# Pooled attention and mixture of depths on one core: steps of 256 tokens instead of 192, and the schedule rebuilt around them

## The chip, the core and the metric

The kernel runs on one core of a Trainium2 chip. The metric is the device time of one execution in microseconds (us), as the median of several runs. A profile of one execution is read beside it: for every engine it has each instruction with its start, its length and what the engine waited for. The engines are named as the profile names them: PE is TensorE's matmul and PEld its weight load, DVE is VectorE, ACT is ScalarE, POOL is GpSimd and SP is SyncE, which here only starts transfers. Each engine works through its own list of instructions in the order in which the program issues them.

## The reference

Eight batches are computed, each with eight heads, 576 tokens and 64 elements per head. The first half is attention against keys and values that were averaged over eight neighbouring tokens, so there are only 72 keys. The second half picks the 128 tokens of a batch with the highest gate score and puts those rows through two dense layers.

```python
def _attn_ref(q, k, v):                       # q, k, v: (8, 8, 576, 64) float32
    k_p = k.reshape(B, H, Sp, 8, D).mean(axis=3)          # Sp = 72
    v_p = v.reshape(B, H, Sp, 8, D).mean(axis=3)
    scores = scale * np.matmul(q, k_p.transpose(0, 1, 3, 2))
    attn = softmax(scores)                    # over the 72 keys
    return np.matmul(attn, v_p)               # bridged to x: (8, 576, 512)

def _moe_ref(x, w_gate, w1, w2, capacity):    # w1: (512, 1024), w2: (1024, 512), capacity 128
    scores = np.einsum('bsd,d->bs', x, w_gate)
    out = x.copy()
    for b in range(B):
        top_idx = np.argpartition(-scores[b], capacity)[:capacity]
        xe = x[b, top_idx]
        ye = np.maximum(xe @ w1, 0.0) @ w2
        g = 1.0 / (1.0 + np.exp(-scores[b, top_idx]))
        out[b, top_idx] = x[b, top_idx] + g[:, None] * ye
    return out
```

## The kernel before

The program has one path that does the work (`direct_path`) and a general one behind a flag, which these inputs do not take. The direct path cuts each batch into nine tiles of 64 tokens and walks through them in steps of three tiles (192 tokens), so there are three steps per batch and 24 in all. One output chunk has 128 rows, which is two tiles, so one step completes one or two chunks.

All matmuls are float32. In the trace one float32 matmul shows as two PE records, and the counts below are of records. Scores of one step: four row groups of 32 partitions, each with its own PSUM bank.

```python
def scores(u):
    b = u // NTH
    p = [bank(i, [128, 2, TS * TL]) for i in range(4)]
    for s in range(2):
        for j in range(2):
            for i in range(4):
                r = slice(32 * i, 32 * i + 32)
                nc.tensor.matmul(p[i][:, s, :], KT[b][r, j, s, :], QT[u][r, j, :, G * s : G * s + G], ...)
    ET[u] = [work.tile([128, 2, TS * TL], FT, name=f"et{i}", bufs=3) for i in range(4)]
    for i in range(4):
        nc.scalar.activation(ET[u][i], p[i], AF.Exp, scale=exp_scale)

def attend(a, heads=range(H)):                # one chunk: 8 heads x 2 tiles
    ...
            nc.tensor.matmul(PA[a][TL * t : TL * t + TL, g, E * n : E * n + E],
                             ET[u][h // 2][:, h % 2, TL * i : TL * i + TL], VP[u // NTH][:, h, :], ...)

def norm(a):                                  # DVE: reciprocal, scaled copy, gate parts
    nc.vector.reciprocal(rz, o[:, :, :, D])
    ...                                       # XS (rows to store, work.tile with 2 buffers), SS (gate parts)
```

Keys and values are pooled on POOL for all batches after the first. `VP` has two buffers, `vps[b % 2]`.

```python
def pool_v(b, g, eng):                        # eng is nc.gpsimd for b > 0
    eng.tensor_tensor(out=x[:, :, 0:4, :], in0=x[:, :, 0:4, :], in1=x[:, :, 4:8, :], op=OP.add)
    eng.tensor_tensor(out=x[:, :, 0:2, :], in0=x[:, :, 0:2, :], in1=x[:, :, 2:4, :], op=OP.add)
    eng.tensor_tensor(out=VP[b][:, h, 0:D], in0=x[:, :, 0, :], in1=x[:, :, 1, :], op=OP.add)
    nc.gpsimd.tensor_tensor(out=x[:, :, 2, :], in0=VP[b][:, h, 0:D], in1=wg[:, h, :], op=OP.mult)

def gate_v(b, g):                             # one more column of VP
    nc.vector.tensor_reduce(out=VP[b][:, h, D + 1], in_=VR[b, g][:, :, 2, :], axis=AX.X, op=OP.add)
```

The selection of a batch is a chain: `row_bcast` (PE), `count` (DVE), `one_hot` (PE, DVE), `gather` (PE, DVE, then an indirect DMA that POOL issues and that reads rows of `out` which the stores have put there), `x_trans` (PE), `hidden` in three parts, `finish` in three parts, and an indirect DMA from POOL that writes the rows back.

```python
def finish(b, part, nb):
    c = slice(176 * part, min(176 * part + 176, DM))
    for f in range(FB):
        nc.tensor.matmul(p, HT[b][:, f, :], w2[:, f, c], start=(f == 0), stop=(f == FB - 1))
    nc.scalar.activation(Y[b][:, c], p, AF.Copy, scale=g)
    nc.gpsimd.tensor_tensor(out=Y[b][:, c], in0=Y[b][:, c], in1=XR[b][:, c], op=OP.add)
    if part == 2:
        i = nc.gpsimd.indirect_dma_start(out=out_rows, out_offset=..., in_=Y[b], in_offset=None)
```

All loads and all stores are issued from SP. A table says in which slot of which step each job is issued; the pooling of the next batch ends one step before it is used, and the last part of `finish` is issued after it.

```python
    at(w + 5, 6, finish, b, 2, 1)             # w = 3 * (b + 1)
    if b + 1 < B:
        u = NTH * b
        at(u, 2, pool_k, b + 1, nc.gpsimd)
        at(u, 5, pool_v, b + 1, 0, nc.gpsimd)
        at(u + 1, 2, pool_v, b + 1, 1, nc.gpsimd)
        at(u + 1, 3, k_trans, b + 1)
        at(u + 2, 2, gate_v, b + 1, 0)
        at(u + 2, 3, gate_v, b + 1, 1)
    ...
for u in range(NU + 6):
    run(u, 0)
    ...                                       # attend and norm of the first chunk
    run(u, 1)
    if 0 < u < NU - 1:
        scores(u + 1)
    ...                                       # attend and norm of the second chunk
    run(u, 2)
    if u + 2 < NU:
        q_trans(u + 2)
    for slot in range(3, 8):
        run(u, slot)
```

Of the kernel before, what the change touches and what calls it, by code (L numbers as in the profile page):

```python
# [48 lines left out]
def direct_path(ctx, tc, q, k, v, moe_w_gate, moe_w1, moe_w2, moe_capacity, out, flag):  # L49
# [20 lines left out]

    nc = tc.nc
# [7 lines left out]
    NT = S // TL  # L79
    QT4 = TL // G  # L80
    TS = 3
    NTH = NT // TS
# [11 lines left out]
    NU = B * NTH  # L94
    NCH = B * NT // 2

# [20 lines left out]

    nc.vector.memset(vraws[0], 0.0)
    nc.gpsimd.memset(vraws[1], 0.0)
# [10 lines left out]
    load_q(0)  # L130
    load_v(0, 0)
# [23 lines left out]
    for t in kts + vps + vraws[2:]:  # L155
        nc.gpsimd.memset(t, 0.0)
    diff = counted("diff", [C, C], [[1, C]], 0, -1)
    part = counted("part", [C, 1], [[0, 1]], 0, 1)
    steps = counted("steps", [C, C // G - 1], [[-G, C // G - 1]], -G, 1)
    numbers = counted("numbers", [C, NC - 1], [[1, NC - 1]], 0, 0)  # L160
# [12 lines left out]
    auxb = [const.tile([C, NC, 5], BF, name=f"auxb{i}") for i in range(2)]  # L173
# [3 lines left out]
    def constants():  # L177
        nc.vector.tensor_scalar(ident, diff, 0.0, None, op0=OP.is_equal)
        nc.vector.tensor_scalar(before[:, NC - 2, :], diff, 0.0, None, op0=OP.is_lt)
        nc.vector.memset(ones, 1.0)  # L180
        nc.vector.memset(one32, 1.0)

        ge, q16, q4, hi = (const.tile([C, n], FT, name=x) for x, n in (
            ("ge", C // G - 1), ("q16", 1), ("q4", 1), ("hi", 1)))
        nc.vector.tensor_scalar(ge, steps, 0.0, None, op0=OP.is_ge, op1=OP.add, accum_out=q16)
        nc.vector.tensor_scalar(q4, q16, 4.0, None, op0=OP.mult)
        nc.vector.scalar_tensor_tensor(hi, q16, -float(G), part, op0=OP.mult, op1=OP.add)
        nc.vector.tensor_scalar(hi, hi, float(TG), None, op0=OP.mult)
        for i, a in enumerate(auxb):
            nc.vector.tensor_scalar(a[:, 0 : NC - 1, 0], numbers, 0.0, hi, op0=OP.mult, op1=OP.add)  # L190
            nc.vector.tensor_copy(a[:, NC - 1, 0:1], hi)
            nc.vector.tensor_scalar(a[:, i : i + NC - 1, 1], numbers, q4, None, op0=OP.add)  # L192
            h = (NC - 1) * (1 - i)
            nc.vector.tensor_scalar(a[:, h, 1:2], q16, float(32 - 4 * i), None, op0=OP.add)
# [10 lines left out]
    def bank(i, shape):  # L205

        return psum.tile(shape, FT, name=f"bank{i}", bufs=1)
# [22 lines left out]
    def pool_v(b, g, eng):  # L230
        x = VR[b, g]
        VP[b] = vps[b % 2]
        h = slice(HG * g, HG * g + HG)
        if eng is nc.vector:
            eng.tensor_reduce(out=VP[b][:, h, 0:D], in_=x.rearrange("p h t d -> p h d t"), axis=AX.X, op=OP.add)
        else:
            eng.tensor_tensor(out=x[:, :, 0:4, :], in0=x[:, :, 0:4, :], in1=x[:, :, 4:8, :], op=OP.add)  # L237
            eng.tensor_tensor(out=x[:, :, 0:2, :], in0=x[:, :, 0:2, :], in1=x[:, :, 2:4, :], op=OP.add)  # L238
            eng.tensor_tensor(out=VP[b][:, h, 0:D], in0=x[:, :, 0, :], in1=x[:, :, 1, :], op=OP.add)

        nc.gpsimd.tensor_tensor(out=x[:, :, 2, :], in0=VP[b][:, h, 0:D], in1=wg[:, h, :], op=OP.mult)
# [7 lines left out]
    QT, ET, PA, XS, SS = {}, {}, {}, {}, {}  # L249

    def tiles_of(b, th):

        full = [slice(i, 32, 4) for i in range(NC - 1)]
        half = slice(32, TG)
        first, second = (slice(i, i + 16, 4) for i in (0, 16))
        shift = lambda s, i: slice(s.start + i, s.stop, 4)
        if b % 2 == 0:
            parts = ((full[0], shift(first, 1)), (shift(second, 1), full[2]), (full[3], half))
        else:
            parts = ((half, full[0]), (full[1], shift(first, 2)), (shift(second, 2), full[3]))  # L260
        return parts[th]

    def q_trans(u):

        b, th = divmod(u, NTH)
        QT[u] = work.tile([128, 2, TS * QT4, 32], FT, name="qt")
        n = 0
        for s in tiles_of(b, th):
            x = QR[b][:, s, :].rearrange("p t (j e) -> p t j e", e=32)
            m = x.shape[1]  # L270
            nc.vector.transpose(out=QT[u][:, :, n : n + m, :].rearrange("p j t c -> p t j c"), in_=x)  # L271
            n += m

    def scores(u):
        b = u // NTH
        p = [bank(i, [128, 2, TS * TL]) for i in range(4)]
        for s in range(2):
            for j in range(2):
                for i in range(4):
                    r = slice(32 * i, 32 * i + 32)  # L280
                    nc.tensor.matmul(p[i][:, s, :], KT[b][r, j, s, :], QT[u][r, j, :, G * s : G * s + G],  # L281
                                     start=(j == 0), stop=(j == 1))
        ET[u] = [work.tile([128, 2, TS * TL], FT, name=f"et{i}", bufs=3) for i in range(4)]
        for i in range(4):
            nc.scalar.activation(ET[u][i], p[i], AF.Exp, scale=exp_scale)  # L285

    def attend(a, heads=range(H)):
        if heads[0] == 0:
            PA[a] = psum.tile([C, 2, 512], FT, name="pA")
        for h in heads:  # L290
# [626 lines left out]
```

## Time and profile before

| | |
|---|---|
| time, median of 3 runs | 276.96 us (276.59 to 277.03) |
| span of the profiled execution | 270.6 us (its device time 272.41 us, mean granted TensorE clock 0.925) |
| PE busy | 223.3 us, 83% of the span |
| DVE / ACT / POOL busy | 137.6 / 66.5 / 155.1 us |
| moved by DMA | 46.94 MB, 173 GB/s over the span |

A busy share is an average over the whole span. The page also cuts the span into 40 slices of 6.8 us and gives the busy tenths of each slice, so one can see where an engine is full and where it is not. The chain that ended last follows the program backwards from its last instruction and names at each step what that step had waited for; in order of time it shows which engine held up the others. A group line gives the busy time of one kind of instruction, the mean length of one in ns, and the idle time of the engine just before these instructions with what ended it. Numbers such as L440 are lines of the kernel.

### The profile page before, as it was taken

Reading aid. Unit: us, or ns where it says so; the run is one execution under the profiler, and the core shown is the slowest. Engines: PE = TensorE matmul, PEld = TensorE weight load, DVE = VectorE, ACT = ScalarE, POOL = GpSimd, SP = SyncE. Lnnn points to the kernel's source line nnn. Section 1 sums busy time; section 2 is a strip of 40 time slices with the busy share of each in tenths; the row PEclk is TensorE's granted clock in tenths of the full one; section 3 lists DMA queues with packets and bytes.
Section 4 is the critical chain, followed back from the end, with each engine's and each line's share of the span. In section 5 each row is a group of like instructions: output and inputs, shape, how many; then the busy total and the mean of one; then the engine's idle time right before and its main releaser. Section 6 shows DMA issues by size and latency. Waiting matters only on the chain.

```text
span 270.6 us, 7289 instructions
## 1 busy us (share of the span) xinstructions
PE 223.3 (83%) x3050; PEld 207.3 (77%) x3050; DVE 137.6 (51%) x387; ACT 66.5 (25%) x162; POOL 155.1 (57%) x193
## 2 busy tenths in 40 slices
PE   0396176680699999999999999999999999999970
PEld 0376165580599799889997998899889999999970
DVE  7859936664064537654755476538554733411000
ACT  2042022211033133323332333223322331212210
POOL 9889706967970229973995299639953103313021
PEclk9999669656589999999999999999999999999995
DMA  7999997876702636686736276831222203301101
GB/s 278 344 354 398 398 354 284 323 274 204 277 13 50 236 88 206 226 263 208 271 65 249 79 217 224 267 95 44 48 71 79 80 18 116 104 2 39 41 0 51
DMA packets 13048, 46.94 MB, mean 173 GB/s; under 512 B 1104, under 2 KB 1104, under 8 KB 10960
## 3 DMA queue, kind: packets, MB, share of 16 engines
q1 hardware_dynamic: 11728, 42.21, 46.1%
q0 software_dynamic: 1280, 4.20, 4.7%
q8 instruction: 26, 0.43, 0.7%
q14 instruction: 14, 0.11, 0.1%
HBM read 34.87 MB, written 11.53 MB: 171 GB/s over the span
## 4 chain that ended last, share of the span: by engine, by line
PE 69%; DVE 13%; DMA 8%; issue 4%; POOL 3%; ACT 0%; POOLq 0%; DVEq 0%
PE bank L452 21%; PE bank L440 18%; PE bank L281 14%; PE pA L294 13%; DMA out_dram<-xs 5%; DVE qt L271 3%; DMA xr<-out_dram,idx 3%; DVE oh L397 2%; PE bank L371 2%; PE bank L428 2%; DVE xs L311 1%; DVE auxb L192 1%; DVE vp L203 1%; PE bank L405 1%; DVE ge L386 1%
## 5 line engine op out<-in xcount | busy, mean ns | idle before, releaser
L281 PE MATMUL bank<-qt,kt 32*128 32x192 f32 x768 | 46.6, 380 | 18.3 <-DVE qt L271 11.7
L440 PE MATMUL bank<-xg,w 128*128 128x128 f32 x512 | 60.5, 277 | 0.0
L452 PE MATMUL bank<-w,ht 128*128 128x176 f32 (+1 forms) x384 | 60.2, 311 | 0.0
L285 ACT ACTIVATE et<-bank 128x384 f32<-128x384 f32 x96 | 39.4, 495 | 81.9 <-PE bank L281 81.9
L440 PEld LDWEIGHTS bank<-xg,w 128*128 128x128 f32 x512 | 58.4, 192 | 0.5 <-ACT et L285 0.5
L452 PEld LDWEIGHTS bank<-w,ht 128*128 128x128 f32 x384 | 55.8, 190 | 0.6
L294 PEld LDWEIGHTS pA<-vp,et 128*64 128x64 f32 x1152 | 42.4, 152 | 15.7 <-issue 14.9
L281 PEld LDWEIGHTS bank<-qt,kt 32*128 32x128 f32 x768 | 38.6, 216 | 20.6 <-POOL sc L168 11.2
L294 PE MATMUL pA<-vp,et 128*64 128x66 f32 x1152 | 49.0, 241 | 6.1 <-DVE rzall L303 4.7
L303 DVE RECIPROCAL rzall<-pA 128x8 f32<-128x8 f32 x36 | 7.5, 207 | 80.3 <-PE pA L294 80.3
L237 POOL TENSOR_TENSOR vraw<-vraw 128x1024 f32<-128x1024 f32 x15 | 35.3, 2354 | 0.9 <-DVE qt L271 0.9
L454 POOL TENSOR_TENSOR y<-y,xr 128x176 f32<-128x176 f32 (+1 forms) x24 | 13.1, 548 | 39.4 <-ACT y L453 39.0
L271 DVE STREAM_TRANSPOSE qt<-qraw 128x512 f32<-128x512 f32 (+1 forms) x48 | 24.5, 551 | 0.0
L442 ACT ACTIVATE ht<-bank 128x384 f32<-128x384 f32 (+1 forms) x24 | 10.9, 456 | 51.9 <-PE bank L440 51.9
L311 DVE TENSOR_TENSOR xs<-pA,rzall 128x512 f32<-128x512 f32 x32 | 22.1, 691 | 1.4 <-DVE rzall L303 0.2
L453 ACT ACTIVATE y<-bank,g 128x176 f32<-128x176 f32 (+1 forms) x24 | 9.7, 403 | 51.2 <-PE bank L452 51.2
L409 POOL TENSOR_SCALAR idx<-tok 128x1 int32<-128x1 f32 x8 | 1.9, 244 | 31.6 <-DVE g L411 31.4
L238 POOL TENSOR_TENSOR vraw<-vraw 128x512 f32<-128x512 f32 x15 | 19.1, 1272 | 1.2
L386 DVE SCALAR_TENSOR_TENSOR ge<-bank,sc,before 128x128 bf16<-128x128 f32 (+3 forms) x40 | 18.2, 498 | 1.6 <-PE bank L371 1.6
L216 POOL TENSOR_TENSOR kraw<-kraw 128x1152 f32<-128x1152 f32 x7 | 18.4, 2634 | 0.1
L362 POOL CAST auxb<-sc 128x5 bf16<-128x5 f32 x8 | 1.6, 202 | 21.1 <-DVE sc L358 10.7
L428 PE MATMUL bank<-ident,xr 128*128 128x128 f32 x32 | 5.3, 292 | 9.2 <-DMA xr<-out_dram,idx 9.2
(85 smaller groups left out, 186.0 us busy)
## 6 DMA issues: line engine op xcount, KB each, us to landing
kraw<-in_k_dram SPq DMA_DIRECT2D x8, 1152.0 KB
qraw<-in_q_dram SPq DMA_DIRECT2D x8, 1152.0 KB
vraw<-in_v_dram SPq DMA_DIRECT2D x16, 512.0 KB
out_dram<-xs SPq DMA_DIRECT2D x16, 512.0 KB
w<-in_moe_w_dram SPq DMA_DIRECT2D x2, 2048.0 KB
vraw<-in_v_dram SPq DMA_DIRECT2D x16, 64.0 KB
out_dram<-xh SPq DMA_DIRECT2D x8, 128.0 KB
wg<-in_moe_w_gate_dram SPq DMA_DIRECT2D x1, 256.0 KB
```

The lines of the kernel that those rows point to most:

```text
L216: eng.tensor_tensor(out=x[:, :, 0:2, :], in0=x[:, :, 0:2, :], in1=x[:, :, 2:4, :], op=OP.add)
L237: eng.tensor_tensor(out=x[:, :, 0:4, :], in0=x[:, :, 0:4, :], in1=x[:, :, 4:8, :], op=OP.add)
L238: eng.tensor_tensor(out=x[:, :, 0:2, :], in0=x[:, :, 0:2, :], in1=x[:, :, 2:4, :], op=OP.add)
L271: nc.vector.transpose(out=QT[u][:, :, n : n + m, :].rearrange("p j t c -> p t j c"), in_=x)
L281: nc.tensor.matmul(p[i][:, s, :], KT[b][r, j, s, :], QT[u][r, j, :, G * s : G * s + G], start=(j == 0), stop=(j == 1))
L285: nc.scalar.activation(ET[u][i], p[i], AF.Exp, scale=exp_scale)
L294: nc.tensor.matmul(PA[a][TL * t : TL * t + TL, g, E * n : E * n + E], ET[u][h // 2][:, h % 2, TL * i : TL * i + TL], VP[u // NTH][:, h, :] ...
L311: nc.vector.tensor_tensor(out=XS[a][:, 0 if XS.get(a - 1) is not XS[a] else 1, :].rearrange("p (g n d) -> p g n d", g=2, d=D), in0=o[:, :, ...
L386: nc.vector.scalar_tensor_tensor(x, y, s, m, op0=OP.is_ge, op1=OP.mult, accum_out=CN[b][:, c : c + 1])
L440: nc.tensor.matmul(p[:, n, :], w1[:, d, 128 * f : 128 * f + 128], XG[b][:, d, :], start=(d == 0), stop=(d == DB - 1))
L452: nc.tensor.matmul(p, HT[b][:, f, :], w2[:, f, c], start=(f == 0), stop=(f == FB - 1))
L454: nc.gpsimd.tensor_tensor(out=Y[b][:, c], in0=Y[b][:, c], in1=XR[b][:, c], op=OP.add)
```

## The change

The change rebuilds the steps and the schedule:

- A step has 256 tokens, so a batch has two of them, and both of its chunks are attended one right after the other. The ninth tile of 64 tokens that is left of each batch makes a step of its own, shared by two neighbouring batches (batches 0 and 1 have one each). There are 21 steps.
- The exponentials of a step are written chunk by chunk: eight instructions of 256 elements take the place of four of 384.
- The dense layers are cut into halves where they were cut into thirds, and `finish` ends with one DVE instruction per half where ACT and POOL had one each.
- The gate is recomputed from the gathered rows on DVE; the three bfloat16 pieces of the score that POOL prepared for the gather are gone.
- Stores are issued from ACT instead of SP; the loads of the weights come later in SP's list.
- Clearing, constants and first pooling are dealt out anew between ACT, POOL and DVE.
- The selection, the dense parts and the pooling have new places in the schedule.

The diff, cut to its core:

```diff
-    TS = 3
-    NTH = NT // TS
+    TM = 4 * QT4
 ...
-    nc.gpsimd.memset(vraws[1], 0.0)
+    for t in vraws[1:]:
+        nc.scalar.memzero(t.rearrange("p h t d -> p (h t d)"))
 ...
+    for b in range(0, B, 2):
+        add_step(b, 0)
+        add_step(b, 1)
+        if b == 0:
+            add_step(None, b, None)
+        else:
+            add_step(None, b, b + 1)
+        add_step(b + 1, 0)
+        add_step(b + 1, 1)
+        if b == 0:
+            add_step(None, None, b + 1)
 ...
+        if b is None:
+            ET[u] = [work.tile([128, 2, len(parts), TL], FT, name=f"el{i}{len(parts)}") for i in range(4)]
 ...
+        else:
+            ET[u] = [[work.tile([128, 2, C], FT, name=f"et{i}{c}") for i in range(4)] for c in range(2)]
+            for c in range(2):
                 for i in range(4):
 ...
+                    nc.scalar.activation(y, x, AF.Exp, scale=exp_scale)
 ...
+                XS[u] = work.tile([C, 2, DM], FT, name="xs", bufs=3)
 ...
-            ins = nc.sync.dma_start(out=rows, in_=x)
+            ins = nc.scalar.dma_start(out=rows, in_=x)
 ...
     def row_bcast(b):
-        SR[b] = [bank(0, [C, NC - 1, C]), bank(1, [C, 1, C])]
+        p = accumulator()
 ...
     def gate(b):
+        nc.vector.scalar_tensor_tensor(Y[b], XR[b], 1.0, wg[:cap].rearrange("p h d -> p (h d)"), op0=OP.mult, op1=OP.mult,
+                                       accum_out=g)
         nc.scalar.activation(g, g, AF.Exp, scale=-1.0)
 ...
-        c = slice(176 * part, min(176 * part + 176, DM))
+        c = slice(DM // 2 * part, DM // 2 * part + DM // 2)
 ...
-        nc.scalar.activation(Y[b][:, c], p, AF.Copy, scale=g)
-        nc.gpsimd.tensor_tensor(out=Y[b][:, c], in0=Y[b][:, c], in1=XR[b][:, c], op=OP.add)
-        if part == 2:
+        nc.vector.scalar_tensor_tensor(Y[b][:, c], p, g, XR[b][:, c], op0=OP.mult, op1=OP.add)
+        if part == 1:
             i = nc.gpsimd.indirect_dma_start(
 ...
+    def dense(b, i, first=False):
+        p = accumulator()[...] if first else bank([128, FB // 2, cap])
+        (hidden, finish)[i // 2](b, i % 2, p)
 ...
+    pool = nc.gpsimd
+    for b, (steps_of, dense_of) in {
+        0: (((2, 1), (3, 0), (3, 3), (5, 0)), ((5, 3, False), (5, 3, False), (6, 1, True), (7, 1, True))),
+        1: (((5, 1), (6, 0), (6, 3), (7, 3)), ((8, 1, True), (9, 1, True), (9, 2, False), (10, 1, True))),
+    }.items():                                # row_bcast and count, one_hot, gather, x_trans; four dense parts
 ...
+    for e in range(2, B, 2):
+        s = 6 + 5 * (e // 2 - 1)              # e at steps s, s+1; ninth tiles s+2; o = e + 1 at s+3, s+4
+        o, last = e + 1, e + 2 == B
+        for f in (row_bcast, count):
+            at(s + 2, 1, f, e)
+            at(s + 4, 0 if last else 1, f, o)
+        at(s + 3, 0, one_hot, e)
+        at(s + 3, 3, gather, e)
+        at(s + 4, 3, x_trans, e)
+        at(s + 4, 3, gate, e)
 ...
+            at(s + 5, 0, one_hot, o)
+            at(s + 5, 3, gather, o)
+            at(s + 6, 3, x_trans, o)
+            at(s + 6, 3, gate, o)
+            for i in range(4):
+                at(s + 5 + i // 2, 1 + i % 2, dense, e, i, i % 2 == 0)
+            at(s + 7, 2, dense, o, 0)
+            at(s + 8, 1, dense, o, 1, True)
+            at(s + 8, 2, dense, o, 2)
+            at(s + 9, 2, dense, o, 3)
 ...
+            x, y = e + 2, e + 3
+            at(s + 2, 4, pool_k, x, pool)
+            at(s + 2, 4, pool_v, x, 0, pool)
+            at(s + 3, 4, pool_v, x, 1, pool)
+            at(s + 4, 4, gate_v, x, 0)
+            at(s + 4, 4, gate_v, x, 1)
+            at(s + 4, 4, pool_k, y, pool)
+            at(s + 5, 4, pool_v, y, 0, pool)
+            at(s + 6, 4, pool_v, y, 1, pool)
+            at(s + 6, 4, gate_v, y, 0)
+            at(s + 6, 4, gate_v, y, 1)
 ...
+    at(2, 0, gate_v, 1, 0)
+    at(2, 0, gate_v, 1, 1)
+    at(3, 4, pool_v, 2, 0, pool)
+    at(4, 1, pool_v, 2, 1, pool)
+    at(5, 4, pool_k, 3, pool)
+    at(6, 4, pool_v, 3, 0, pool)
+    at(7, 1, pool_v, 3, 1, pool)
+    at(7, 4, gate_v, 3, 0)
+    at(7, 4, gate_v, 3, 1)
 ...
+    for u in range(NU + 1):
+        for a, x in enumerate(chunks):
+            if x[0] == u:
+                attend(a)
+                norm(a)
         run(u, 0)
 ...
+        if u + 1 < NU:
             scores(u + 1)
 ...
+        if u < NU:
+            store_x(u)
         if u + 2 < NU:
             q_trans(u + 2)
+        for slot in range(1, 5):
             run(u, slot)
```

## The prediction

> **What bounds the kernel now.** I read the 40 slices first:
>
> ```profile
> PE   0396176680699999999999999999999999999970
> PEclk9999669656589999999999999999999999999995
> ...
> DMA  7999997876702636686736276831222203301101
> ```
>
> PE is full from slice 11 (about 75 us) to slice 38, at an open clock. Before that it is patchy and slow: the front is bound by something else. The chain in order of time says by what:
>
> ```profile
> 29.21 0.12 DVE rzall L303
> 29.36 0.69 DVE xs L311
> 30.05 0.03 DVE ss L314
> 30.07 13.98 DMA out_dram<-xs
> ...
> 58.47 3.45 issue
> 61.92 8.24 DMA xr<-out_dram,idx
> 70.16 0.14 issue
> 70.29 1.09 PE bank L428 x4
> ```
>
> A store issued at 30.07 lands after 13.98 us, behind loads on the same queue; the first gather, which reads stored rows, starts at 61.92 and lands at 70.16. From 70.3 PE works almost without a gap until its last dense record ends at about 262.4: 192.1 us. The chain then ends with the scatter at 270.6. One period, from the same view:
>
> ```profile
> 184.46 5.62 PE bank L440 x48
> 190.08 1.09 PE pA L294 x32
> 191.17 1.51 PE bank L281 x32
> 192.68 1.11 PE pA L294 x32
> ...
> 195.87 0.83 DVE oh L397
> 196.70 0.04 issue
> 196.75 0.28 PE bank L405 x5
> 197.03 2.49 PE bank L452 x16
> ```
>
> Hidden parts begin at 77.26 and, five batches on, at 211.92: 26.9 us a batch. Once a batch DVE (L397) sets the pace and PE idles about 0.6 us. Last, the timeline of POOL:
>
> ```profile
> 208.06 0.52 POOL L454 TENSOR_TENSOR y<-y,xr 128x160 f32<-128x160 f32 x1 [1.86 <-ACT y L453]
> 208.86 1.09 POOL L456 DMA_INDIRECT out_dram<-y,idx  x1 [0.29 <-POOL y L454]
> 209.96 0.22 POOL L362 CAST auxb<-sc 128x5 bf16<-128x5 f32 x1
> ```
>
> POOL waits for the last part of finish, spends 1.09 us on the scatter, and only then takes what stands behind it. That order is the heart of what follows.
>
> **What the Trainium skill says.** "DMA: Bandwidth & Descriptors", Queues, rings and completion order: SP and ACT each own one ring per DMA engine, and an engine takes turns between rings. So a store on ACT's ring no longer stands behind SP's loads; the 13.98 us above agree with its first half, the second no trace here shows yet. "PSUM — Partial Sum Buffer", Engine vs sequencer instructions: the ACT, DVE and POOL queues are strictly first in, first out; the POOL lines agree. "TensorE: Matmul & The Clock Gate", Part 1: an idle window of some 3.4 us halves PE's clock, and it takes about as long to come back. It agrees: after the 9.2 us gap before 70.29 four transposes take 1.09 us where 0.44 is usual, one step's scores 2.87 for 1.51, and until 77 about 3.1 us are lost.
>
> **The change, part by part.**
>
> *PE work.* First a check that the 192.1 us are understood: dense 8 x (64 x 0.112 + 7.32) = 115.9, 17 steps of scores at 1.51, 27 chunks at 1.14, row_bcast, one-hot and gather 1.4 for seven batches, transposes 0.44 for eight, 3.1 for the cold start and 3.6 of one-hot idling come to 192.4. Now the changes. 48 hidden records (128 columns) take 5.36 us, 112 ns each; 32 of finish (176 columns) 4.79, 150 ns: 0.8 ns per column. A half of 256 columns costs 112 + 128 x 0.8 = 214 ns, 32 of them 6.85 us against 2.49 + 2.65 + 2.18 = 7.32: -0.47 a batch, -3.8 in all. Scores of 192 columns: 32 records in 1.51 us, 189 ns per pack of four row groups; 64 columns more give 240, so 8 x 240 = 1.92 us for a full step. The 64-column step of a batch would be 0.7 us by columns, but the attention records never run closer than 1.09/32 = 34 ns, so 32 x 34 = 1.1. Per batch 2 x 1.92 + 1.1 = 4.94 against 3 x 1.51 = 4.53; after the first gather twelve full and three double ninth steps are left, 29.6 us, where before it was 17 x 1.51 = 25.7: +3.9 (1.9 of it a step that now falls behind the gather). Attention: the profile has 64 records in a row in 2.02 us and 32 alone in 1.09, about 1.14 per chunk as now split; 27 chunks: 24 x 1.01 + 3 x 1.09 = 27.5 against 30.8: -3.3. The one-hot now stands before scores and dense work and no longer holds PE: -0.6 x 6 = -3.6. Sum: 192.1 - 3.8 + 3.9 - 3.3 - 3.6 = 185.3 us after the first gather.
>
> *The front.* I walk through the lists. DVE pools keys and values of batch 0 itself; scores(0) about 12.6, attention from about 18. POOL then pools batch 1: 2.6 + 1.4 for keys, twice (2.35 + 1.27 + 0.73 + 0.68) = 5.0 for values, from 18 to about 32.5. DVE waits for that in step 2 (gate_v), then counts (4 us, to 38), normalises two chunks (2.4), builds the one-hot (1.0) and the gather issues at about 44.5. Stores of batch 0 leave on ACT by 36 and have landed. The gather lands 3.4 to 8.2 us after issue (median 4.3); loads still run, so I take 8: first transposes at 52.5 instead of 70.3, **17.8 us sooner**. The queue change and the third xs buffer pay here only.
>
> *New waits.* Each comes from an order of issue.
>
> 1. pool_v(y, 1) stands in slot 4 of step s+6, behind the last finish half of batch e in slot 2, whose scatter POOL issues. The ninth step s+7 begins at once with attend on y and needs it. Counted from the end of that finish half: DVE 0.5, hand-over 0.3, scatter 1.1, three additions 4.5, product 0.7, gate_v 0.5 = 7.7 us. PE has one transpose group (0.44) and half a chunk (0.5): it idles **about 6.9 us**. This comes at steps 13 and 18, and at step 8 by the same rule (scatter of batch 0 ahead of pool_v(3, 1) in one slot). The clock then falls; the gap before 70.29 cost 3.1, so I take 2.5 for each: 3 x 9.4 = 28.2.
> 2. gate_v(x) at the end of step s+4 stands behind finish and gate on DVE: 0.5 + 0.8 + 0.8 against 0.44 of PE work, 1.6 us at steps 11 and 16: 3.2.
> 3. A dense half in bank 0 right after scores waits for the exponentials: 384 elements take 495 ns and follow at 410; 256 should follow at about 300, so bank 0 is free after five, 1.5 us, with 0.7 of row_bcast between: about 0.9, four times: 3.7.
> 4. one_hot waits for its accumulator while the first norm reads it: 0.3 x 6 = 2.
>
> With the cold start after the first gather (3.0, paid before too and in the 192.1; not added): 28.2 + 3.2 + 3.7 + 2 = 37.1.
>
> *The tail.* One DVE instruction (0.45) for ACT 0.40 and POOL 0.56: 7.6 instead of 8.2.
>
> *Sum.* 52.5 + 185.3 + 37.1 + 7.6 = 282.5 us of span. The timed median is 276.96 - 270.6 = 6.4 above the span now; I take 5, as a less filled PE leaves less to vary: 287.5, **287 us**.
>
> **The rivals.**
>
> *A: PE stays the bound and the front's gain stands.* Without wait 1: 282.5 - 28.2 + 5 = 259 us. For it: PE is full after 75 us now, the change lowers its work, and POOL is busy only 57%. Against: the share is an average; the wait is one of order, not of load. It would be right if POOL's list were not in the order I read, or if the scatter were issued elsewhere.
>
> *B: the front does not move.* If the gather still lands near 65 (by the lengths above I count some 42 us of DVE work in the first 50, and its instructions stretch beside POOL: L192 took 2.24 us against 0.14), add 12: about 299. The slices of DMA are full up to slice 7, so loads and stores compete.
>
> *C: ACT becomes the bound.* Eight exponentials of about 300 ns, two store issues of 0.65 and two relus of 0.49 make 4.7 us in a step of 11.7; ACT is busy 25% now. I see nothing for it.
>
> *D: DVE becomes the bound.* It takes over gate and finish and loses the score sums: about 36 of 51 us per pair of batches. It only matters through waits 1 and 2.
>
> **Range and chances.** The front is uncertain by 5 us either way, each of the three long waits by 2 (6 together), the small ones by 4; in quadrature about 9. That gives 276 to 297 around 287. Rival A reaches 259; I give the reading of POOL's order 85%, so the low end goes down to 268, and the high end is 298. Faster than 271.4: mostly rival A, 0.15. Within 2%: the low half of my own range, 0.2. Slower than 282.5: 0.65.
>
> **What would show it.** The first x_trans (four transposes of xr) starts near 52 instead of 70.3. In the waits, PE's attention matmuls wait for DVE's gate_v reduce three times, 6 to 7 us each, at roughly 84, 146 and 211 us, with PEclk falling to 5 or 6 there, and POOL shows scatter, three additions and product back to back in each gap. Scores show about 1.9 us per 32 records of 256 columns, finish 214 ns per record. Wrong would be: no such gaps (rival A), a first gather after 60 (rival B), gaps of PE that end with ACT (rival C).

## Result and profile after

The changed kernel takes 307.11 us (median of 4, 305.86 to 307.29) where the kernel before, run beside it, took 277.00 us: a ratio of 1.108, 95% interval 1.105 to 1.111. It is 30 us slower. The prediction said 287 us, with 268 to 298 as its range: the direction was right, the size was not.

The 40 slices of the changed kernel, each 7.6 us of a span of 305.4 us:

```profile
PE   0488565389992979949992799789982799799990
PEclk9999977559997799977997599999997899999997
```

Before, PE was a row of nines from slice 11 on. Now there are holes in slices 12, 21 and 30 (the first slice is 0) and a smaller one in slice 17, and the clock drops at each of them. POOL, at 43% of the span, is less busy than before (57%), but a share of the whole span does not show whether POOL is full at the holes; experiment 1 tests that.

The table of stretches sizes the loss. Each line is one stretch from the first transposes of gathered rows to PE's last dense work: its length, then busy time of PE, PEld, DVE, ACT and POOL with their instructions, then mean granted clock, DMA share and GB/s. First the kernel before:

```profile
70.30:262.40 192.10, 189.04 (x2513) 177.07 (x2513) 90.95 (x279) 53.02 (x130) 101.70 (x129) 0.98 0.40 124
```

then the changed kernel:

```profile
57.80:297.30 239.50, 201.67 (x2415) 179.76 (x2415) 99.93 (x317) 56.13 (x140) 92.71 (x75) 0.91 0.33 111
```

The gather arrives 12.5 us earlier, and the stretch behind it is 47.4 us longer. Of its 239.5 us PE idles 37.8 (3.1 before), and its clock averages 0.91. In the clock record of this trace the values are full and half only; half falls, within the stretch, at 57.8 to 68.9, 96.2 to 103.0, 133.7 to 140.5, 164.4 to 174.7 and 232.7 to 239.5, which is 41.8 us.

What PE waited for, from the waits of the changed kernel (total us, times, longest one):

```profile
PE pA L352 <- DVE vp L256: 25.8, 8, 5.9
...
PE pA L352 <- DVE ge L432: 4.7, 2, 2.9
```

The first is attention waiting for gate_v, the second attention waiting for count; 1.5 and 2.9 us of them stand ahead of the first gather. The three longest waits for gate_v, at steps 8, 13 (in two parts) and 18 (not shown, 0.82 and 5.61), on PE's timeline with the idle time in brackets:

```profile
99.38 1.14 PE L352 MATMUL pA<-vp,el 128*64 128x66 f32 x14 [5.88 <-DVE vp L256]
...
162.53 0.69 PE L352 MATMUL pA<-vp,el 128*64 128x66 f32 x16 [0.82 <-DVE vp L256]
168.82 1.14 PE L352 MATMUL pA<-vp,el 128*64 128x66 f32 x14 [5.60 <-DVE vp L256]
```

How the longest kind comes about is in the chain in order of time, here at step 13:

```profile
157.56 3.47 PE bank L502 x16
...
161.05 0.49 DVE y L503
...
161.81 1.22 POOL out_dram L505
...
163.07 2.34 POOL vraw L248
...
165.49 1.27 POOL vraw L249
...
166.83 0.73 POOL vp L250
...
167.63 0.69 POOL vraw L252
...
168.34 0.43 DVE vp L256
...
168.82 1.14 PE pA L352 x14
```

One chain, with no gap wider than 0.3 us: the last finish half on PE, its end on DVE, the scatter on POOL, three additions and the product of pool_v, gate_v on DVE, and only then the second half of the attention chunk. PE had been ready since 163.2.

### The profile page after: what moved, and what is told of

It reads as the page before. It is cut to its first block, busy times and chain, and to the rows that moved or that the text cites. A ratio compares the mean times of both kernels' runs of the same rounds, so it can differ in the third digit from the quotient of the medians.

```text
span 305.4 us, 7024 instructions
## 1 busy us (share of the span) xinstructions
PE 232.1 (76%) x2922; PEld 205.4 (67%) x2922; DVE 139.3 (46%) x416; ACT 76.9 (25%) x185; POOL 130.7 (43%) x135
## 4 chain that ended last, share of the span: by engine, by line
PE 54%; POOL 13%; issue 11%; DVE 10%; DMA 8%; ACT 2%; ACTq 1%; POOLq 0%; DVEq 0%; SPq 0%
PE bank L502 13%; PE bank L323 11%; PE pA L489 9%; PE bank L489 8%; PE pA L352 8%; POOL vraw L248 4%; PE pA L502 4%; DMA qraw<-in_q_dram 3%; DMA xr<-out_dram,idx 2%; POOL vraw L249 2%; DMA out_dram<-xs 2%; ACT et L338 2%; DVE ge L432 1%; POOL vp L250 1%; DVE kh L236 1%
## 5 line engine op out<-in xcount | busy, mean ns | idle before, releaser
L338 ACT ACTIVATE et<-bank 128x256 f32<-128x256 f32 x128 | 49.0, 535 | 104.6 <-PE bank L323 104.6
L323 PE MATMUL bank<-qt,kt 32*128 32x256 f32 (+1 forms) x768 | 51.5, 412 | 13.9 <-DVE qt L308 12.1
L352 PEld LDWEIGHTS pA<-vp,et 128*64 128x64 f32 x1024 | 36.7, 152 | 16.5 <-DVE vp L256 6.0
L502 PE MATMUL bank<-w,ht 128*128 128x256 f32 x176 | 39.7, 380 | 1.7 <-ACT et L338 1.7
L489 PE MATMUL bank<-xg,w 128*128 128x128 f32 x288 | 35.3, 284 | 4.5 <-ACT et L338 3.8
L489 PEld LDWEIGHTS bank<-xg,w 128*128 128x128 f32 x288 | 34.2, 199 | 5.7 <-ACT et L338 4.8
L502 PEld LDWEIGHTS bank<-w,ht 128*128 128x128 f32 x176 | 32.9, 190 | 6.1 <-ACT et L338 1.9
L489 PEld LDWEIGHTS pA<-xg,w 128*128 128x128 f32 x224 | 25.5, 192 | 3.0 <-issue 2.0
L489 PE MATMUL pA<-xg,w 128*128 128x128 f32 x224 | 26.9, 278 | 0.7 <-ACT xg L481 0.7
L503 DVE SCALAR_TENSOR_TENSOR y<-bank,g,xr 128x256 f32<-128x256 f32 x11 | 5.3, 484 | 48.3 <-PE bank L502 48.3
L308 DVE STREAM_TRANSPOSE qt<-qraw 128x1024 f32<-128x1024 f32 (+1 forms) x24 | 23.0, 968 | 0.1
L502 PE MATMUL pA<-w,ht 128*128 128x256 f32 x80 | 18.6, 386 | 0.0
## 6 DMA issues: line engine op xcount, KB each, us to landing
out_dram<-xs ACTq DMA_DIRECT2D x32, 256.0 KB, 4.1
wg<-in_moe_w_gate_dram SPq DMA_DIRECT2D x1, 256.0 KB, 7.6
```

What stands on the lines that cost most here:

```text
L308: nc.vector.transpose(out=QT[u][:, :, n : n + x.shape[1], :].rearrange("p j t c -> p t j c"), in_=x)
L323: nc.tensor.matmul(p[i][:, s, n, :], KT[x][r, j, s, :], QT[u][r, j, t, G * s : G * s + G], start=(j == 0), stop=(j == 1))
L338: nc.scalar.activation(y, x, AF.Exp, scale=exp_scale)
L489: nc.tensor.matmul(p[:, n, :], w1[:, d, 128 * f : 128 * f + 128], XG[b][:, d, :], start=(d == 0), stop=(d == DB - 1))
L502: nc.tensor.matmul(p, HT[b, n][:, m, :], w2[:, f, c], start=(f == 0), stop=(f == FB - 1))
```

## Experiments

Falls are measured from the changed kernel's 307.11 us, which repeated within 1 us (experiment 9). The kernel before has shorter executions of 268 to 271 us and longer ones of 273 to 277, so the ratios to it below compare shorter ones alone; the 277.00 above is of the longer kind, and against the shorter the changed kernel, run again, takes 1.135 times as long (1.123 to 1.146).

**1. Only POOL's order (e1_pool_order).**

```diff
-            at(s + 6, 4, pool_v, y, 1, pool)
+            at(s + 6, 0, pool_v, y, 1, pool)
 ...
-    at(7, 1, pool_v, 3, 1, pool)
+    at(7, 0, pool_v, 3, 1, pool)
```

> Edit to the changed kernel: the second half of the value pooling, pool_v(y, 1) and pool_v(3, 1), is issued in slot 0 of its step, ahead of the last finish half and so ahead of its scatter on POOL; nothing else moves. Theory (order on POOL): the three long waits at steps 8, 13 and 18 (5.9, 6.4 and 6.4 us idle, and about 28 us in all with the slow clock after them) shrink to 1.5 to 2.5 us each, because gate_v still stands behind finish and gate on DVE. The time falls by 18 to 27 us, from 307 to 280-289, and the records of attention in those steps start within 3 us of the end of the work before. Rival (POOL's load, not its order, holds the values back): POOL has no spare time before the scatter, the additions end at the same moment, and the time falls by less than 8 us.

Measured: 292.38 us, 14.7 less. In steps 13 and 18 the theory held in full. The timeline of PE in this run:

```profile
95.00 0.69 PE L352 MATMUL pA<-vp,el 128*64 128x66 f32 x16 [2.19 <-DVE vp L256]
97.80 1.14 PE L352 MATMUL pA<-vp,el 128*64 128x66 f32 x14 [2.11 <-DVE vp L256]
...
163.62 1.34 PE L352 MATMUL pA<-vp,el 128*64 128x66 f32 x30 [0.86 <-DVE vp L256]
```

At 163.62 the wait is 0.86 us where it was 0.82 + 5.60, and step 18 reads 0.89. At step 8 (95.00 and 97.80) 4.3 of 5.9 us stay, which is why the fall missed the expected 18 to 27: there the place of the scatter cost only 1.6 us. POOL's own timeline says what holds the rest:

```profile
66.69 1.40 POOL L231 TENSOR_TENSOR ks<-kraw 128x576 f32<-128x576 f32 x1
84.58 0.23 POOL L455 TENSOR_SCALAR idx<-tok 128x1 int32<-128x1 f32 x1 [16.49 <-DVE tok L453]
```

POOL stands idle for 16.5 us in front of the second gather's index, with both halves of pool_v(3) queued behind it. So the rival (no room on POOL) is wrong, since POOL had time to spare ahead of this gather, and the theory was too narrow: a gather blocks the pooling behind it as a scatter does.

**2. Stores back on SP (e3_stores_sp).**

```diff
-            ins = nc.scalar.dma_start(out=rows, in_=x)
+            ins = nc.sync.dma_start(out=rows, in_=x)
```

> Edit to the changed kernel: the stores of rows are issued from SP again, behind the loads, and not from ACT; nothing else moves. Theory (what the new queue is worth): the 34 store issues of about 0.6 us leave ACT's list, so the exponentials of a step end up to 1 us earlier and the waits for PSUM banks (about 8 us in all) fall by 3 to 5 us; but the first stores stand behind loads on SP, so the first gather comes later, 3 to 10 us. Sum: between 3 us faster and 7 us slower, first transposes of gathered rows at 61 to 68 instead of 57.8. Rival (queues change nothing, the first gather is held by loads in any case): the first transposes stay within 1 us of 57.8 and the time falls by the 3 to 5 us of ACT.

Measured: 312.06 us, 5 more, with the first transposes at 61.4. PE's waits for exponentials did not shrink (dense for exponentials: "PE bank L489" 4.3 us here, 3.8 in the changed kernel), so the store issues on ACT, though they stand between exponentials, cost PE nothing that shows. The first gather now starts 9.64 us after its index, and the profile ends that wait with the landing of a store. The queue is worth about 5 us to the changed kernel, and 3.6 of the 12.5 us by which its gather comes earlier.

**3. Stores of the kernel before on ACT (b1_before_stores_act).** The same edit the other way round, in the kernel before.

> Edit to the kernel before: only the queue of the stores changes, from SP to ACT; steps of 192 tokens and everything else stay. Theory (the store behind the loads, 13.98 us from 30.07 to 44, was on the path to the first gather): stores land some 5 to 10 us sooner, the first transposes of gathered rows start at 63 to 67 instead of 70.3, and the time falls by 3 to 7 us, less what 48 issues of 0.6 us on ACT cost. Rival (the front of the kernel before was bound by pooling and counting on POOL and DVE, or by the gather's own start): the first transposes stay within 1.5 us of 70.3 and the time stays within 2 us of 277 or rises with the issues on ACT.

Measured: 274.84 us, 1.025 of the kernel before (1.013 to 1.036), first transposes at 70.85 (70.29 before). The gather came no earlier, as the rival has it. The time decides less: 273.8 to 276.1 us lies where the longer executions of the kernel before lie, so a loss is not shown. The edit also moved the issue: on ACT's list the first store stands behind exponentials and is issued at 37.34, on SP's it was at 30.07. From there it still takes 9.97 us to land, with SP's loads under way. The Trainium skill, "DMA: Bandwidth & Descriptors", Queues, rings and completion order, says that an engine takes turns between rings; that may be, but a ring of its own did not make this store quick. The earlier gather of the changed kernel therefore does not come from the queue alone; what brought the rest was not taken apart.

**4. A spare gather ahead (e4_early_gather).** In the changed kernel the first gather starts 5.8 us after its index is ready. POOL's timeline:

```profile
44.82 0.24 POOL L455 TENSOR_SCALAR idx<-tok 128x1 int32<-128x1 f32 x1 [8.42 <-DVE tok L453]
50.85 1.23 POOL L457 DMA_INDIRECT xr<-out_dram,idx  x1 [5.79 <-issue]
```

```diff
+    zero = const.tile([cap, 1], I32, name="zero")
+    spare = work.tile([cap, DM], FT, name="xr", bufs=3)
+    nc.gpsimd.memset(zero, 0)
+    nc.gpsimd.indirect_dma_start(out=spare, out_offset=None, in_=moe_w2,
+                                 in_offset=bass.IndirectOffsetOnAxis(ap=zero[:, :1], axis=0))
```

> Edit to the changed kernel: one spare indirect gather (index zero in all 128 rows, from the weights into a buffer that is free then) is issued from POOL ahead of the pooling of batch 1, about 30 us before the first real gather. It adds 128 rows of 2 KB and one issue of about 1 us. Theory (first-use cost: the first indirect transfer of a program has some 5.8 us on POOL that later ones do not have, the 'issue' gap between 45.0 and 50.85): the gap moves to the spare gather, where it delays the pooling of batch 1; the real gather starts within 1.5 us of its index and lands earlier, first transposes at 52 to 56 instead of 57.8. Rival (the first gather waits for the loads of the weights, whose last one lands at the same 50.85): the gap stays where it is, the first transposes stay within 1 us of 57.8, and the time changes by less than 1.5 us.

Measured: 304.75 us, first transposes at 55.33. The gap is gone (0.66 us), but neither theory had it right: the spare gather itself had no gap (0.30 us). It was not passed on, it vanished, so it is no cost of a first use; and the loads were as before.

**5. Four small instructions ahead (e5_pad).** What the spare gather also did was to move everything behind it along in POOL's list.

```diff
+    pad = const.tile([C, 1], FT, name="pad")
+    for _ in range(4):
+        nc.gpsimd.memset(pad, 0.0)
     pool_k(1, pool)
```

> Edit to the changed kernel: four clearing instructions of one column (0.1 us each) are put on POOL ahead of the pooling of batch 1; no gather is added, nothing else moves. The first gather stood still for 5.4 us between its second and third wait instruction, though every store it waits for had landed, and the spare gather of the run before took the gap away without having one itself. Theory (POOL's list is fetched in pieces of 8 KB, and the boundary of two pieces falls between those two instructions; the fetch, a packet of the instruction queue q14 about 2.1 us before the gather, is asked for only then and stands behind the loads): with four more instructions ahead, the boundary is met while POOL idles from 36.8 on, the gap shrinks to under 1 us, the first transposes start at 51 to 54 instead of 57.8 and the time falls by 3 to 6 us. Rivals (the first indirect transfer of a program costs this, or the stores or loads end only then): the gap stays at 5 us or more and the first transposes stay within 1 us of 57.8.

Measured: the gap is gone again. POOL's timeline in this run:

```profile
46.45 0.24 POOL L455 TENSOR_SCALAR idx<-tok 128x1 int32<-128x1 f32 x1 [9.54 <-DVE tok L453]
47.49 1.23 POOL L457 DMA_INDIRECT xr<-out_dram,idx  x1 [0.80 <-POOL idx L455]
```

Its time, 305.41 us, fell by 1.7 only, under the expected 3 to 6 and hardly more than the changed kernel varies: the index itself came at 46.45, and the first transposes at 55.15, where the two profiles of the changed kernel have them at 57.83 and 58.40. Both rivals are out: neither a first transfer nor the stores could be cured by four clears. (In four other runs with such a gap the profile names a store's landing as its end. But the last stores issued before it, at 42.5 and 43.1 in the changed kernel, are of batch 1, and this gather does not wait for them.) What is left is the position in POOL's list. A packet that fits the theory's fetch is seen in the view of the DMA queues, here of the changed kernel between 48.5 and 49.2 us, where the loads fill the engines:

```profile
q1 hardware_dynamic: 115, 0.28, 100.7%
q10 hardware_dynamic: 18, 0.01, 5.5%
q14 instruction: 1, 0.01, 2.8%
```

In all seven runs of the changed kernel and its variants that had the gap, one such 8 KB packet of the instruction queue came 2.1 to 2.3 us before the gather started (48.70 and 50.85 here; in six of them a second one some 0.6 to 1.3 us earlier). In the five runs without it, no packet stood in that place. The kernel before has one too, at 59.81, 2.1 us ahead of its first gather. The packets do not name their engine, so that this one is POOL's is inferred from the timing and from what the padding did.

**6. Only orders on POOL and DVE (e6_order).** For the periodic part:

```diff
-            at(s + 3, 4, pool_v, x, 1, pool)
-            at(s + 3, 4, k_trans, x)
-            at(s + 4, 4, gate_v, x, 0)
-            at(s + 4, 4, gate_v, x, 1)
-            at(s + 4, 4, pool_k, y, pool)
-            at(s + 5, 4, pool_v, y, 0, pool)
-            at(s + 5, 4, k_trans, y)
-            at(s + 6, 4, pool_v, y, 1, pool)
-            at(s + 6, 4, gate_v, y, 0)
-            at(s + 6, 4, gate_v, y, 1)
+            at(s + 3, 0, pool_v, x, 1, pool)
+            at(s + 3, 1, k_trans, x)
+            at(s + 4, 0, gate_v, x, 0)
+            at(s + 4, 0, gate_v, x, 1)
+            at(s + 4, 0, pool_k, y, pool)
+            at(s + 4, 0, pool_v, y, 0, pool)
+            at(s + 5, 0, pool_v, y, 1, pool)
+            at(s + 5, 1, k_trans, y)
+            at(s + 6, 0, gate_v, y, 0)
+            at(s + 6, 0, gate_v, y, 1)
```

and batches 2 and 3 likewise: pool_v(3, ·) at (5, 4) and (6, 0), k_trans(3) at (6, 1), gate_v(2, ·) at (5, 1) and gate_v(3, ·) at (7, 0).

> Edit to the changed kernel: only orders on POOL and DVE. All pooling of values is issued ahead of the gathers and scatters of its step (so POOL doesn't stand before a gather's index with pooling behind it), gate_v follows one step later right after the normalising, ahead of finish and gate, and k_trans ahead of finish. Moving the second half of the value pooling alone had taken away 14 us of span and had left 4.3 us at step 8, 4.5 at step 11 and 0.9 to 1.1 at steps 13, 16 and 18. Theory (all waits of attention for gate_v are order): the waits of attention matmuls for vp fall from 25.8 us to under 3, the span from 305 to 275 to 282. Rival (POOL or DVE has no room): new waits for vp or for kt of over 2 us each, and the span stays over 286.

Measured: 276.98 us, 30.1 less, as the median of four that spread from 271.94 to 278.79, so the fall is known to 28 to 35 us only. Span 273.4 (305.4 in the changed kernel). In its waits:

```profile
PE pA L352 <- DVE ge L432: 6.5, 3, 3.1
...
PE pA L352 <- DVE vp L256: 1.5, 1, 1.5
```

The wait for the values falls from 25.8 to 1.5 us, and these 1.5 are in the first step, which the edit does not touch; the wait for count grows from 4.7 to 6.5, by 1.58 us at step 11, where it had been hidden. Not one instruction of work was taken out. The theory holds: these waits were order, not load.

**7. Only buffers of the dense halves (e7_acc).** `True` puts a half into an accumulator buffer; without it the half goes to a bank that the exponentials of the scores must free first. Two halves of batch 1 also move behind row_bcast.

```diff
-        0: (..., ((5, 3, False), (5, 3, False), (6, 1, True), (7, 1, True))),
-        1: (..., ((8, 1, True), (9, 1, True), (9, 2, False), (10, 1, True))),
+        0: (..., ((5, 3, True), (5, 3, True), (6, 1, True), (7, 1, True))),
+        1: (..., ((8, 2, True), (9, 1, True), (9, 2, True), (10, 2, True))),
 ...
-                at(s + 5 + i // 2, 1 + i % 2, dense, e, i, i % 2 == 0)
-            at(s + 7, 2, dense, o, 0)
+                at(s + 5 + i // 2, 1 + i % 2, dense, e, i, True)
+            at(s + 7, 2, dense, o, 0, True)
 ...
-            at(s + 8, 2, dense, o, 2)
+            at(s + 8, 2, dense, o, 2, True)
-            at(s + 9, 2, dense, o, 3)
+            at(s + 9, 2, dense, o, 3, True)
```

> Edit to the changed kernel: every dense half goes to an accumulator buffer, none to a bank that the exponentials must free first, and two halves of batch 1 stand after row_bcast instead of before it. Theory (the small waits are of buffers): the waits of dense work for exponentials (1.1 to 1.9 us, four times, about 6) and the two waits of attention for the count (4.7) go; the three long waits for the values stay; the time falls by 6 to 11 us. Rival (accumulators only turn the wait round: attention or one_hot then waits for relu, finish or count): the time falls by less than 3 us and waits for pA appear in the same steps.

Measured: 292.43 us, 14.7 less, more than the expected 6 to 11. Gone are the dense waits for exponentials (1.09, 1.11, 1.67 and 1.59 us, 5.5 in sum) and attention's wait of 1.81 us for count at step 9. At step 11 one line shows a third effect. First the changed kernel, then this run, both from PE's timeline:

```profile
135.64 3.79 PE L352 MATMUL pA<-vp,et 128*64 128x66 f32 x64 [4.47 <-DVE vp L256]
```

```profile
127.44 2.09 PE L352 MATMUL pA<-vp,et 128*64 128x66 f32 x64 [1.17 <-DVE vp L256]
```

With the dense half behind row_bcast, count runs beside it and gate_v is late by 1.17 us only. The wait shrinks by 3.3 us, and the same 64 records then take 2.09 us instead of 3.79: the granted clock was full here and half there. Over the stretch behind the gather, idle time falls by 10.7 us and busy time by 5.0.

**8. The three edits together (v1_all).**

> The three edits of this call together: the padding on POOL, the orders on POOL and DVE, all dense halves in accumulators. If the three causes are separate and are what the changed kernel loses, the falls add up: 5 + 25 + 8 = 38 us from 307, so about 269, close to the kernel before (270 here) and near the 259 that the prediction's rival A gives for a kernel without these waits. If they overlap (one wait hides behind another), the sum of the single falls is not reached and the time stays over 275.

Measured: 258.79 us, 0.960 of the kernel before (0.949 to 0.971). The single falls were 1.7, 30.1 and 14.7, in sum 46.5; together they are 48.3. Within the spread of experiment 6 that agrees, but it does not make the causes separate. Experiments 6 and 7 both shorten the wait at step 11, so it is counted twice; against that, the padding gives more here than alone (3.6 us, experiment 9). The stretch behind the gather in this version:

```profile
54.90:248.00 193.10, 187.41 (x2413) 170.02 (x2414) 98.13 (x317) 56.67 (x140) 92.28 (x75) 0.99 0.42 142
```

PE idles 5.7 of 193.1 us where the changed kernel idled 37.8. The same matmuls keep it busy for 187.4 us where they took 201.7, at a mean clock of 0.99 where it was 0.91.

**9. The changed kernel again, and v1_all without the padding (after_again, e8_nopad).** No edit, and the padding taken out.

> The changed kernel once more, without an edit, beside the others of this call, because the kernel before has read 270 to 277 us from one call to the next. Expected: 305 to 308 us, the three waits for the values at steps 8, 13 and 18 at 5.5 to 6.5 us each, and the gap ahead of the first gather between 5 and 6 us. If it reads under 302, the falls of the single edits were overrated by as much.

> The version with all three edits (258.8 us), less the padding on POOL: orders and accumulators stay. Theory (the fetch of POOL's list costs the first gather 5.4 us, and now that nothing behind it waits, most of that reaches the end): the gap ahead of the first gather is back at 5 to 6 us, the first transposes start at 57 to 59 instead of 54.9, and the time is 2 to 5 us above 258.8. Rival (the padding did nothing but shift, or the gap is luck of one execution): no gap, the time within 1 us of 258.8.

Measured: 306.78 us, with the gap at 5.75 us and waits of 6.2 us in sum at step 8; so the falls above stand. Without the padding v1_all takes 262.40 us, 3.6 more, with the gap back at 5.93 us and the first transposes at 58.55 instead of 54.91. The gap is worth these 3.6 us once the waits behind it are gone.

**10. The front (v2_front).**

```diff
-        0: (((2, 1), (3, 0), (3, 3), (5, 0)),
+        0: (((2, 1), (3, 0), (3, 0), (5, 0)),
 ...
-    at(2, 0, gate_v, 1, 0)
-    at(2, 0, gate_v, 1, 1)
+    at(2, 1, gate_v, 1, 0)
+    at(2, 1, gate_v, 1, 1)
```

> The version with all three edits, plus two orders at the front: the small gather matmuls of batch 0 directly behind its one-hot instead of behind the next scores (they waited 2.3 us for exponentials and 3.2 us for cold scores), and gate_v of batch 1 behind the count of batch 0 instead of ahead of it (the count waited 1.9 us for POOL). Theory (the front is a chain of PE and DVE orders up to the first gather): its index is ready at 40 to 43 instead of 45.9, the first transposes start at 49 to 52 instead of 54.9, and the time falls by 3 to 5 us to 254-256. Rival (the transfer is bound by the loads in the rings): the gather lands at the same moment as before, within 1 us, and the time stays within 1 us of 258.8.

Measured: 253.54 us, 0.940 of the kernel before (0.932 to 0.948), the best version of this study. The index came at 41.74 as expected, and the gather landed at 50.9, after 8.1 us. But the first transposes began only at 53.00, without a wait for it: PE was at attention until then, at half clock until 50.92. The slices of this version:

```profile
PE   0078947888998999999999999999999997998970
PEclk9999965599999999999999999999999999999995
```

From slice 8 on PE is under 8 in slice 33 only until the tail, and the clock stays open.

**11. One load moved out of the way (v3_late_w2).**

```diff
-        nc.sync.dma_start(out=w2, in_=moe_w2.rearrange("(a p) n -> p a n", p=128))
+        nc.scalar.dma_start(out=w2, in_=moe_w2.rearrange("(a p) n -> p a n", p=128))
 ...
-    at(0, 2, load_w2)
+    at(4, 1, load_w2)
```

> The version of the run before, plus one transfer moved: the 2 MB of the second dense layer are loaded from ACT's queue at step 4 instead of from SP's at step 0; they are first needed at about 70 us. Theory (the first gather lands 7 to 8 us after its issue, the others 3.5, because 400 GB/s of loads share the DMA engines with it): it lands 4 to 5 us after issue, the first transposes start 2 to 4 us earlier than without this edit, and the time falls by 1.5 to 3 us more. Rival (other loads move up and fill the same window): the landing still takes over 6.5 us and the time stays within 1 us.

Measured: 256.07 us, 2.5 more. The gather lands 6.7 us after its issue instead of 8.1, but the first transposes start at 53.30, again directly behind attention: PE reaches them no earlier. The theory's premise holds in part, its gain could not come. Whether the kernel became slower is not settled: of the six times of v2_front four are 253.1 to 253.6 us and two 255.7 to 256.0, of this version five are 255.7 to 256.8, and the profiled spans (254.4 and 254.2) are the same because the profile of v2_front is of its 256.0 us.

## Why the prediction was right and where it was wrong

In its own sum the span was 52.5 + 185.3 + 37.1 + 7.6 = 282.5. In the trace it is 57.8 + 239.5 + 8.1 = 305.4. The tail is right within 0.5 us. The step that failed is the term for the new waits, 37.1 us: its mechanism was right, its size was not, because waits off the regular period and the slow clock behind them were left out. Behind the gather the prediction had 29.6 us of idle time (3 x 6.9, 3.2, 3.7 and 2) and 192.8 of work (185.3 and 7.5 for the clock); the trace has 37.8 and 201.7. That is 17.1 us of the 22.9 by which the span was missed; the front is 5.3. Step by step:

**PE's work: right.** 185.3 us were predicted for the stretch behind the gather; v1_all is busy 187.4 in it. The sizes hold: a full step of scores takes 1.94 to 2.01 us (1.92), a finish half at open clock 3.47 (3.42). A hidden half takes 3.77 where 32 records of 112 ns make 3.58, so a batch was put 0.37 too low; the line of 48 records that the prediction shows has 5.62 us, its sum took the 5.36 of others.

**New wait 1: right at steps 13 and 18, right in size only at step 8.** Three waits of about 6.9 us idle were predicted (its terms add up to 7.6, not 7.7, and leave 6.7). They measured 5.9, 6.4 and 6.4. At step 8 the scatter made 1.6 of the 5.9 us; the rest came from the gather of batch 1, behind which both halves of pool_v(3) stood (experiment 1), and the prediction did not have it. Behind the three waits PE worked 3.6, 5.9 and 4.2 us at half clock. By half of that, an estimate, they cost 6.8 us more: 25.5 in all, where 28.2 were predicted. Experiment 6, which removed waits 1 and 2 by order alone, returned 30.1 us; the prediction had 28.2 + 3.2 = 31.4 for the two, in part by luck, as wait 1 was put too high and wait 2 too low.

**New wait 2: under-sized at one place.** 1.6 us at steps 11 and 16 were predicted; 1.08 came at step 16, but 4.47 at step 11. There the last dense half of batch 1 stands ahead of row_bcast, so DVE comes to count, gate and gate_v late. The prediction had taken the order of the periodic steps for all steps.

**New wait 3: under-sized.** 3.7 us for four places; 5.5 in idle time. The prediction let bank 0 come free 1.5 us after the first exponential begins. At step 15 it took 2.3 us: the first begins at 196.45, the dense half at 198.74. The last five exponentials are 0.29 us apart, as estimated, but beside two store issues it is about 0.45. With the stores on SP (experiment 2) eight of them took 3.05 us where they took 3.06, some 0.36 apart, so the estimate of 0.3 was too low either way.

**New wait 4: over-sized.** 2 us; four waits of 0.18 us came.

**Waits not listed: 7.1 us.** Attention for count (1.81), the second gather (0.87), k_trans behind finish (1.04), the copies of the transposes (2.14) and row_bcast behind the last normalisations (1.24).

**The clock: charged for too few gaps.** 2.5 us for each of three waits was about right (2.3). But behind the 4.47 us wait at step 11 the clock was at half as well, for 4.9 us of work, and the cold start after the first gather lasted to about 69 us. In all the work took 14.3 us longer than in v1_all, where the prediction had 7.5 beyond the cold start it counted. The Trainium skill, "TensorE: Matmul & The Clock Gate", Part 1, whose idle window of some 3.4 us the prediction cited, would have said so: 4.47 is longer than that. These runs do not show it as a sharp limit: in e6_order a wait of 1.80 us at step 9 was followed by half clock for 3.4 us, in the changed kernel a wait of 1.81 us there was not. So the term for the waits, 37.1 us, was mis-sized, though each wait that it named was there: by difference to v1_all, which still idles 5.7 us, it is 239.5 - 193.1 = 46.4 us.

**The front: wrong by 5.3.** The index was ready at 44.8, where 44.5 was predicted for the issue. The landing took 7.0 us (8). In between lay the gap of 5.8 us, and the line "3.45 issue" ahead of the first gather in the profile before was in the very fence that the prediction showed. It was not asked about.

**From span to time:** 5 us were added, and 1.7 were due. The 6.4 us on which the 5 rest are a median of 276.96 less the span of one execution, which itself took 272.41, 1.8 us above its span.

**The rivals.** A was wrong for this kernel, but its 259 us is where the work lies once the waits are gone: v1_all takes 258.8. To get there all the waits and the gap had to go, not wait 1 alone, so the agreement is partly luck. B's 299 us lies nearer to the measured time, but its reason fits badly: the gather came at 57.8, not after 60. For C and D no long wait of PE was found that ends with ACT or DVE being full; the waits on DVE were of order.

## What to carry to other kernels

An engine that works through its list in order blocks what stands behind an instruction that waits, however idle the engine is: ahead of each scatter, gather or other waiting instruction, issue what others need next. Price a wait of PE together with the slow clock behind it, and count every gap, also those off the regular period. A gap marked "issue" ahead of a single instruction deserves a question of its own, because its cost repeats in no other place and can sit on the path.

## What the runs showed of the hardware

- The profile counts packets of an "instruction" kind on the DMA queues. One of 8 KB preceded the first gather by 2.1 to 2.3 us in each of seven runs with a gap (5.75 to 5.93 us in six, 9.64 with the stores on SP), and four clears of 0.14 us placed earlier made the gap vanish. That the gap is POOL's wait for this packet is inferred.
- The first store took 9.97 us to land from ACT's queue and 13.98 from SP's, both beside loads; the issue on ACT came 7.3 us later, so the two are not the same moment.
- The same 64 attention records took 3.79 us at half clock, after a wait of 4.47 us, and 2.09 at full clock, after one of 1.17.
